# A forward Fourier step split 49 by 64 instead of 98 by 32, with products on quarters of TensorE's array

## The chip, the cores and the metric

One core of a Trainium2 chip runs the whole program. The metric is the device time of one execution in microseconds; lower is better. TensorE (PE in the profile) multiplies matrices, its weight loads are listed as PEld; VectorE is DVE, ScalarE is ACT, GpSimd is POOL, and SyncE (SP) issues all DMAs of this kernel.

## The reference

Eight sequences of 3136 rows and 256 columns go through a Fourier layer and then, row by row, through a two-matrix layer with a softmax-weighted activation. Cut to what matters:

```python
X = np.fft.rfft(x, axis=1)                       # x: (8, 3136, 256), along the 3136 rows
Yr = Xr @ w_r - Xi @ w_i + b_r
Yi = Xr @ w_i + Xi @ w_r + b_i
Y  = soft_threshold(Yr, 0.01) + 1j * soft_threshold(Yi, 0.01)
x  = np.fft.irfft(Y, n=3136, axis=1).reshape(25088, 256)
h  = x @ w_in                                    # w_in: 256 x 1024
solu = h * softmax(h)
ln = (solu - mean(solu)) / sqrt(var(solu) + 1e-6) * g_ln
out = ln @ w_out                                 # w_out: 1024 x 256
```

## The kernel before

The transform of one sequence is made of matrix products. The 3136 row numbers are split in two factors, and the forward part has two steps: step 1 transforms along the first factor, its result goes through DRAM (`s1`), and step 2 applies the second factor together with the twiddles. Then the mixing with `w_r` and `w_i` follows (`mix`), the inverse step 1 (`inv1`), DRAM again (`s2`), and the inverse step 2 (`inv2`), which writes columns of 98 rows into a ring in SBUF (`ring_hi`, `ring_lo`). From the ring, tiles of 128 rows are taken by the second layer: `moe_head` (first product, softmax), `moe_turn` (split into two float16 parts and transposes by DMA, `th<-lh` and `tl<-ll`) and `moe_tail` (second product, `po`, and the output).

Numbers are held as pairs of float16, high and low, and a product is three matmuls: high by high, high by low, low by high. Only the first sequences are treated otherwise: step 1 and 2 of sequences 0 and 1 are in float32 (`fwd1_plain`).

In step 1 a sequence is eight chunks of four values of the second factor, 98 rows by 1024 elements. `fwd1` loads one chunk (`xt`, one DMA of 98 rows of 4 KB), splits it in `xh` and `xl` (ScalarE, VectorE), and for each half of 512 columns makes three matmuls of 98 rows into one PSUM bank. ScalarE and VectorE bring each bank to SBUF as the pair `av`, and one DMA of 98 rows of 4 KB stores it. Before its eight chunks a sequence is read once more in eight loads of 128 rows for the largest absolute value (`load_peak`, `set_scales`). `xt` has four buffers, shared by both.

`inv1` already works on halves of the array: its weights `gb` have 64 rows, and the two products of a pair of frequencies stand on the two row halves.

Nothing in the program runs in the order of the text. `Plan` records every operation with a key, and `order` builds the order of each engine's queue: at each point it takes, of the operations that could start within 50 ns of the first, the one with the smallest key. It works with lengths for each operation (`weigh`), a single transfer bus and a fixed charge for entering and leaving a split array. All operations of the kernel are issued at one line, so in the profile nearly everything stands at L342, and groups are told apart by the tiles' names (`fa_s` there is also `fa16_s`, since digits are left out). Keys count tiles of the second layer. The main loop has, for each sequence `b`, 24 or 25 such tiles; beside them it spreads the front of sequence `b + 2` (`front_a`: peaks, scales, `fwd1`) and the second half of the front of `b + 1` (`front_b`: `fwd2`, `mix`, `inv1`):

```python
if b + 2 < B:
    front_a(b + 2, first + 6, (L - 6) / 17)
if b + 1 < B:
    front_b(b + 1, first + (6 if b == 0 else 0), (L - (8 if b == 0 else 2)) / (NU + 3))
```

At the start nothing else can run: sequence 0 goes through `fwd1_plain` in eight chunks, all are stored, and `fwd2` begins when its first `bin` has been loaded back.

Of the kernel before, what the change touches and what calls it, by code (L numbers as in the profile page):

```python
# [25 lines left out]
H = N1 // 2  # L26
Q = (H - 1) // 2
# [5 lines left out]
S_SCALE, B_SCALE, Z_SCALE, X_SCALE = 2.0**-7, 2.0**-5, 2.0**-11, 2.0**-11  # L33
# [6 lines left out]
def fft_constants():  # L40

    FA, IA = np.zeros((N1, N1)), np.zeros((N1, N1))
    comps = []
    for q in range(Q):
        comps += [(2 * q + 1, 0), (2 * q + 2, 0), (2 * q + 1, 1), (2 * q + 2, 1)]
    comps += [(0, 0), (H, 0)]  # L50
    for c, (k1, im) in enumerate(comps):
        t = 2 * np.pi * ((np.arange(N1) * k1) % N1) / N1
        FA[:, c] = -np.sin(t) if im else np.cos(t)
        IA[c, :] = (1.0 if k1 in (0, H) else 2.0) / S * (-np.sin(t) if im else np.cos(t))

    def angle(k):
        return 2 * np.pi * ((np.arange(N2)[:, None] * np.asarray(k)[None, :]) % S) / S

    P = 4 * N2
    FB, GB = np.zeros((P, Q, P)), np.zeros((P, Q, P))  # L60
    for q in range(Q):
        for j in range(2):
            k = 2 * q + 1 + j + N1 * np.arange(N2)
            s = np.where(2 * k > S, -1.0, 1.0)[None, :]
            C, Sn = np.cos(angle(k)), np.sin(angle(k))
            re, im = slice(j * N2, (j + 1) * N2), slice((2 + j) * N2, (3 + j) * N2)
            FB[re, q, re], FB[im, q, re] = C, Sn
            FB[re, q, im], FB[im, q, im] = -Sn * s, C * s
            GB[re, q, re], GB[im, q, re] = C.T, -(Sn * s).T
            GB[re, q, im], GB[im, q, im] = Sn.T, (C * s).T  # L70
    kd, kn = N1 * np.arange(1, N2 // 2), H + N1 * np.arange(N2 // 2)
    nd, m = len(kd), len(kd) + len(kn)
    FS, GS = np.zeros((2 * N2, P)), np.zeros((P, 2 * N2))
    d, n, I = slice(0, N2), slice(N2, 2 * N2), 2 * N2
    alt = np.cos(np.pi * np.arange(N2))
    FS[d, 0:nd], FS[n, nd:m], FS[d, m], FS[d, m + 1] = np.cos(angle(kd)), np.cos(angle(kn)), 1.0, alt
    FS[d, I : I + nd], FS[n, I + nd : I + m] = -np.sin(angle(kd)), -np.sin(angle(kn))
# [12 lines left out]
    out = dict(fa=FA.astype(np.float32), fbf=FB.astype(np.float32), fsf=FS.astype(np.float32))  # L90
    out["iaf"] = (IA * IA_SCALE).astype(np.float32)
    parts = dict(fa16=FA * A_SCALE, fb=FB, fs=FS, gb=GB * G_SCALE, gs=GS * G_SCALE, ia=IA * IA_SCALE)
# [132 lines left out]
class Op:  # L225
    def __init__(self, engine, key, seq):
        self.engine, self.key, self.seq = engine, key, seq
        self.calls, self.length, self.moved, self.tiles = [], 0.0, 0.0, []
        self.needs, self.next, self.start, self.end, self.half, self.port = set(), [], None, None, False, False
# [7 lines left out]
class Plan:  # L237
# [60 lines left out]
    def weigh(self, op, name, args, kw, ins, outs):  # L298
# [45 lines left out]
    def order(self):  # L344
        ready = {e: [] for e in self.ENGINES}
        free = dict.fromkeys(self.ENGINES, 0.0)
        waits, bus, half, port = {}, 0.0, False, 0.0
# [35 lines left out]
        while len(done) < len(self.ops):  # L383
# [68 lines left out]
def fft_mix_solu_kernel(ctx: ExitStack, tc, x, w_r, w_i, b_r, b_i, w_in, w_out, g_ln, fa, fbf, fsf, iaf, fa16, fb, fs, gb, gs, ia, out):  # L452
# [70 lines left out]

    def load_after(t, src, before):
# [56 lines left out]
    def fwd1(b, c):  # L581
        if c == 0:
            s1[b] = dram.tile([N1, N2, 2, D], F16, name="s1")
        xt = xp.tile([P, C1], F32, name="xt", bufs=4)[:N1]
        nc.sync.dma_start(xt, x[b].rearrange("(n1 n2) d -> n1 (n2 d)", n1=N1)[:, c * C1 : (c + 1) * C1])
        xh = xp.tile([N1, C1], F16, name="xh")
        xl = xp.tile([N1, C1], F16, name="xl")
        k = scales[b]["x"][:N1]
        nc.scalar.activation(xh, xt, AF.Copy, scale=k)
        nc.vector.scalar_tensor_tensor(xl, xt, k, xh, ALU.mult, ALU.subtract)  # L590
        n2 = C1 // D
        av = xp.tile([P, n2, 2, D], F16, name="av")[:N1]
        for h in range(C1 // HF):
            hs = slice(h * HF, (h + 1) * HF)
            pa = front_psum(b)
            nc.reserve(av[:, h * HF // D : (h + 1) * HF // D])
# [3 lines left out]
            pv = pa[:N1].rearrange("p (n d) -> p n d", d=D)  # L600
            ah, al = (av[:, h * HF // D : (h + 1) * HF // D, j] for j in range(2))
# [6 lines left out]
    def fwd1_plain(b, c):  # L608


        if c == 0:
            s1[b] = dram.tile([N1, N2, D], F32, name="s1f")
        n2 = C1 // D
        pool, name, bufs = (mp, "u", 4) if b == 0 and c % 2 == 0 else (xp, "xt", 4)
        xt = pool.tile([P, C1], F32, name=name, bufs=bufs)[:N1]
        if b and c < 4:
# [18 lines left out]
        for av, i, n in parts:  # L635
            nc.sync.dma_start(s1[b][:, c * n2 + i : c * n2 + i + n], av.rearrange("p (n d) -> p n d", d=D))
# [8 lines left out]
    def load_bin(b, g):  # L645

        if b >= PLAIN:
            v = s1[b][: 4 * Q].rearrange("(q c) n t d -> q c n (t d)", c=4).rearrange("q c n m -> (c n) q m")
# [3 lines left out]
        v = s1[b][: 4 * Q].rearrange("(q c) n d -> q (c n) d", c=4).rearrange("q r d -> r q d")  # L652
# [15 lines left out]
    def fwd2(b, u):  # L668
# [3 lines left out]
        if n == 1:  # L672
            if b >= PLAIN:
                bt, gi, fw = fp.tile([K, 1, 2, D], F16, name="bin_s", bufs=1), 0, [fs_s]
                nc.sync.dma_start(bt[:, 0], s1[b][4 * Q :].rearrange("c n t d -> (c n) t d"))
            else:
                bt, gi, fw = fp.tile([K, 1, D], F32, name="bin_s", bufs=1), 0, [fsf_s]
                nc.sync.dma_start(bt[:, 0], s1[b][4 * Q :].rearrange("c n d -> (c n) d"))
# [353 lines left out]
    fa16_s = load([N1, 2, N1], fa16, "fa16_s", dtype=F16)  # L1032
# [132 lines left out]
    for b in range(B):  # L1165
        tiles = range(0, 24) if b % 2 == 0 else range(24, 49)
        L = len(tiles)
        if b == 0:
            front_a(1, -40, 0.5)
        if b + 2 < B:  # L1170
            front_a(b + 2, first + 6, (L - 6) / 17)
        if b + 1 < B:
            front_b(b + 1, first + (6 if b == 0 else 0), (L - (8 if b == 0 else 2)) / (NU + 3))
        groups = 0
        for n, t in enumerate(tiles):
            need = min((t + 1) * P - (b % 2) * S, S)
            while groups < N2 // G2 and groups * G2 * N1 < need:
                nc.key = first + n - 2
# [6 lines left out]
            nc.key = first + n + 1  # L1185
# [30 lines left out]
```

## Time and profile before

| what | value |
|---|---|
| median of 3 runs | 1636.32 us (1631.87 to 1637.99) |
| the profiled execution | 1638.51 us |
| its span, first to last instruction | 1636.7 us |
| TensorE busy | 1586.2 us, 97% |
| VectorE busy | 1317.3 us, 80% |
| ScalarE busy | 1234.6 us, 75% |
| GpSimd busy | 1129.3 us, 69% |
| DMA: time of packets, share of 16 engines | 80.9% |
| mean granted TensorE clock | 0.986 |

The span is cut in 40 slices of 40.9 us in the page; a digit is the busy share of a slice in tenths. A matmul's duration in the lists runs past the start of the next one, so the cost of a stream of matmuls is read from the distances of their starts. A row of a window gives its length, the busy time and count of each engine, the granted clock, the DMA share and GB/s.

### The profile page before, as it was taken

How to read it: one execution, taken by the hardware profiler on the slowest of the kernel's cores; microseconds unless marked ns; L12 is line 12 of the kernel's file. 1: busy time of each engine (PE TensorE's matmuls, PEld its weight loads, DVE VectorE, ACT ScalarE, POOL GpSimd, SP SyncE). 2: the span in 40 equal slices, each digit the busy share in tenths (PEclk: the TensorE clock that was granted, in tenths of full speed). 3: DMA queues.
4: the chain of work that ended last, by engine and by line, in shares of the span. 5: the costliest groups of instructions: out<-in, count | busy, mean ns of one | idle time of the engine just before them, and what ended most of it. 6: DMA issues, size and time to landing. Idle time of an engine off the chain costs nothing.

```text
span 1636.7 us, 37871 instructions
## 1 busy us (share of the span) xinstructions
PE 1586.2 (97%) x13040; PEld 1127.8 (69%) x13040; DVE 1317.3 (80%) x3343; ACT 1234.6 (75%) x2496; POOL 1129.3 (69%) x1889
## 2 busy tenths in 40 slices
PE   6979999999999999999999999999999999999998
PEld 3545877676775787668766677766877677676675
DVE  4778779985888867997799977899689877777774
ACT  4667678885788767887678867788678876678786
POOL 0656777676875687768766687766887677776775
PEclk8989999999999999999999999999999999999999
DMA  8868966997669977899758996699767977669776
GB/s 249 274 223 205 194 149 155 229 207 146 151 151 233 214 152 133 189 249 192 162 102 191 251 209 132 134 234 243 162 134 158 191 165 145 119 137 144 150 130 106
DMA packets 532258, 290.23 MB, mean 177 GB/s; under 512 B 425978, under 2 KB 502300, under 8 KB 532064
## 3 DMA queue, kind: packets, MB, share of 16 engines
q1 hardware_dynamic: 532064, 287.81, 80.9%
q8 instruction: 102, 1.67, 0.4%
q14 instruction: 92, 0.75, 0.1%
HBM read 107.89 MB, written 77.07 MB: 113 GB/s over the span
## 4 chain that ended last, share of the span: by engine, by line
PE 78%; DMA 8%; DVE 5%; ACT 3%; POOL 2%; issue 2%; SPq 0%; DVEq 0%; ACTq 0%; POOLq 0%
PE po L342 26%; PE ph L342 24%; PE pf L342 23%; PE pb L342 4%; DMA th<-lh 4%; DMA tl<-ll 3%; DVE u L342 1%; POOL ll L342 1%; ACT junk L342 1%; DVE xl L342 1%; ACT lh L342 1%; DVE nm L342 1%; ACT u L342 0%; DMA zt<-s 0%; DVE av L342 0%
## 5 line engine op out<-in xcount | busy, mean ns | idle before, releaser
L342 POOL TENSOR_TENSOR ll<-u,lh 128x1024 f16<-128x1024 f32 x196 | 427.2, 2180 | 116.0 <-ACT lh L342 110.0
L342 PE MATMUL po<-wout,th 128*128 128x256 f16 x3136 | 375.3, 273 | 10.6 <-DMA th<-lh 9.2
L342 PEld LDWEIGHTS <-th 128*128 128x128 f16 x3136 | 303.8, 98 | 74.5 <-DMA th<-lh 15.8
L342 ACT ACTIVATE u<-ph,m,hsb 128x512 f32<-128x512 f32 x384 | 296.1, 776 | 50.5 <-DVE m L342 46.9
L342 DVE TENSOR_REDUCE nm<-ph 128x1 f32<-128x512 f32 x392 | 265.0, 684 | 82.3 <-PE ph L342 80.7
L342 DVE SCALAR_TENSOR_TENSOR u<-ph,ch,u 128x512 f32<-128x512 f32 x392 | 281.6, 747 | 31.1 <-ACT u L342 20.0
L342 PE MATMUL ph<-win_hi,ring_hi 128*128 128x512 f16 x784 | 298.2, 380 | 1.3 <-DVE ring_lo L342 0.8
L342 PE MATMUL ph<-win_low,ring_lo 128*128 128x512 f16 x784 | 297.8, 380 | 0.0
L342 PE MATMUL ph<-win_lo,ring_hi 128*128 128x512 f16 x784 | 297.8, 380 | 0.0
L342 ACT CAST lh<-u 128x1024 f16<-128x1024 f32 x196 | 205.3, 1047 | 64.2 <-DVE u L342 57.2
L342 PEld LDWEIGHTS <-ring_hi 128*128 128x128 f16 x1568 | 150.3, 98 | 142.7 <-issue 5.9
L342 ACT ACTIVATE junk<-u,total 128x1024 bf16<-128x1024 f32 x196 | 226.0, 1153 | 13.1 <-POOL total L342 12.8
L342 PE MATMUL po<-wout,tl 128*128 128x256 f16 x1568 | 204.2, 273 | 6.3 <-DMA tl<-ll 6.3
L342 PEld LDWEIGHTS <-tl 128*128 128x128 f16 x1568 | 150.4, 98 | 39.8 <-DMA tl<-ll 8.6
L342 POOL TENSOR_TENSOR y<-yt,yc 128x512 f32<-128x512 f32 (+1 forms) x104 | 133.0, 1279 | 61.0 <-ACT yt L342 32.7
L342 POOL TENSOR_TENSOR yl<-y,yh 128x512 f16<-128x512 f32 (+1 forms) x104 | 127.2, 1224 | 47.6 <-ACT yh L342 47.0
L342 PE MATMUL pf<-w_hi,Xh 128*128 128x256 f16 (+1 forms) x546 | 149.2, 273 | 0.0
L342 PE MATMUL pf<-w_hi,Xl 128*128 128x256 f16 (+1 forms) x546 | 148.8, 273 | 0.0
L342 PE MATMUL pf<-w_lo,Xh 128*128 128x256 f16 (+1 forms) x546 | 148.8, 273 | 0.0
L342 ACT ACTIVATE o<-po,r 128x256 f32<-128x256 f32 x196 | 92.6, 473 | 72.0 <-PE po L342 53.8
L342 PEld LDWEIGHTS <-ring_lo 128*128 128x128 f16 x784 | 76.7, 98 | 93.8 <-DVE ring_lo L342 0.8
L342 PEld LDWEIGHTS <-Xh 128*128 128x128 f16 (+1 forms) x1196 | 114.2, 99 | 27.7 <-issue 3.7
(189 smaller groups left out, 2851.0 us busy)
## 6 DMA issues: line engine op xcount, KB each, us to landing
xt<-in_x_dram SPq DMA_DIRECT2D x108, 392.0 KB
zt<-s SPq DMA_DIRECT2D x56, 392.0 KB
s<-zout SPq DMA_DIRECT2D x42, 512.0 KB
s<-av SPq DMA_DIRECT2D x48, 392.0 KB
bin<-s SPq DMA_DIRECT2D x36, 512.0 KB
out_dram<-o SPq DMA_DIRECT2D x64, 98.0 KB
bin<-s1f SPq DMA_DIRECT2D x12, 512.0 KB
s1f<-av SPq DMA_DIRECT2D x10, 392.0 KB
```

The source lines that it names most:

```text
L342: getattr(engine, name)(*args, **kw)
```

## The change

The forward split becomes 49 by 64; the inverse keeps 98 by 32. Step 1's matrix is 49 by 49. In float32 (`fwd1_plain`) two copies of it stand on the diagonal of a 98 by 98 matrix, so that a matmul still takes 98 rows: two sets of 49. In float16 (`fwd1`) a chunk of 1024 elements is laid on partitions 0 to 48 and 64 to 112, and four products, each of 49 rows into 64 output rows by 512 columns, stand on the four quarters of the array; three rounds of four matmuls fill two PSUM banks, each bank both its halves of partitions. ScalarE and VectorE then work on 113 partitions, with as many instructions as before.

Each load of a chunk and each store becomes two DMAs of 49 rows (in `fwd1` the load has two runs of 2 KB in each row). The x buffers become one constant tile of four places: in the float16 stages places 0 and 1 for `fwd1`, 2 and 3 for the peaks; partitions 32 to 63 of the first two are cleared once (`clear_between`). Step 2 keeps its sizes: a group is now two components by 64 values, not four by 32. In the planner the array may be split in 1, 2 or 4, and four keys change.

```diff
-S, N1, N2 = 3136, 98, 32
-H = N1 // 2
-Q = (H - 1) // 2
+F1, F2 = N1 // 2, 2 * N2
+Q = (F1 - 1) // 2
...
-            op.half = "gb" in ins[0].tile.kw["name"]
-            op.length += n / 2 if op.half else n
+            op.split = {"gb": 2, "fa16_s": 4}.get(...)
+            op.length += n / op.split
...
-                if op.half != half:
-                    at += 100.0 if op.half else 220.0
-                half = op.half
+                if op.split != split:
+                    at += 100.0 if split == 1 else 220.0
+                split = op.split
...
+    places = const.tile([P, 4, C1], F32, name="xt")
...
+    def clear_between():
+        nc.gpsimd.memset(places[P // 4 : P // 2, :2], 0.0)
...
-        t = xp.tile([P, C1], F32, name="xt", bufs=4)[:, :n]
+        t = x_place(2, 3)[:, :n]
...
     def fwd1(b, c):
-        xt = xp.tile([P, C1], F32, name="xt", bufs=4)[:N1]
-        nc.sync.dma_start(xt, x[b].rearrange("(n1 n2) d -> n1 (n2 d)", n1=N1)[:, c * C1 : (c + 1) * C1])
+        half = P // 2
+        R = half + F1
+        xt = x_place(0, 1)[:R]
+        xv = x[b].rearrange("(n1 c g r i) d -> c r n1 g (i d)", n1=F1, g=2, r=2, i=2)
+        for r in range(2):
+            nc.sync.dma_start(xt[r * half : r * half + F1].rearrange("p (g m) -> p g m", g=2), xv[c, r])
...
-        for h in range(C1 // HF):
-            pa = front_psum(b)
-            with nc.together():
-                for i, (t, j) in enumerate(((xh, 0), (xh, 1), (xl, 0))):
-                    nc.tensor.matmul(pa[:N1], fa16_s[:, j], t[:, hs], start=i == 0, stop=i == 2)
+        pa = [front_psum(b) for _ in range(2)]
+        with nc.together():
+            for i, (t, j) in enumerate(((xh, 0), (xh, 1), (xl, 0))):
+                for r in range(2):
+                    rows = slice(r * half, r * half + F1)
+                    for g in range(2):
+                        nc.tensor.matmul(
+                            pa[r][g * half : (g + 1) * half], fa16_s[rows, j], t[rows, g * HF : (g + 1) * HF], start=i == 0, stop=i == 2
+                        )
...
-        nc.sync.dma_start(s1[b][:, c * n2 : (c + 1) * n2], av)
+        for g in range(2):
+            nc.sync.dma_start(
+                s1[b][:, 8 * c + 4 * g : 8 * c + 4 * g + 4].rearrange("k n t d -> k (n t d)"),
+                av[g * half : g * half + F1].rearrange("p r i t d -> p (r i t d)"),
+            )
...
     def fwd1_plain(b, c):
-        nc.sync.dma_start(xt, x[b].rearrange("(n1 n2) d -> n1 (n2 d)", n1=N1)[:, c * C1 : (c + 1) * C1])
+        xv = x[b].rearrange("(n1 h c n2) d -> c h n1 (n2 d)", n1=F1, h=2, n2=n2)
+        for h in range(2):
+            nc.sync.dma_start(xt[h * F1 : (h + 1) * F1], xv[c, h])
...
-            nc.sync.dma_start(s1[b][:, c * n2 + i : c * n2 + i + n], av.rearrange("p (n d) -> p n d", d=D))
+            for h in range(2):
+                at = h * N2 + c * n2 + i
+                nc.sync.dma_start(s1[b][:, at : at + n].rearrange("k n d -> k (n d)"), av[h * F1 : (h + 1) * F1])
...
         if b + 2 < B:
-            front_a(b + 2, first + 6, (L - 6) / 17)
+            front_a(b + 2, first + 9, (L - 9) / 17)
         if b + 1 < B:
-            front_b(b + 1, first + (6 if b == 0 else 0), (L - (8 if b == 0 else 2)) / (NU + 3))
+            front_b(b + 1, first + (6 if b == 0 else -0), (L - (8 if b == 0 else 4)) / (NU + 3))
...
-                nc.key = first + n - 2
+                nc.key = first + n - 3
                 inv2(b, groups)
...
-            nc.key = first + n + 1
+            nc.key = first + n + 1.5
             moe_tail(*turned.pop(0))
```

More of the change, by code (lines that the diff above doesn't have):

```diff
@@ L40, in fft_constants, with angle @@
 def fft_constants():
[L46 to L50, printed above, removed]
+    FA, IA = np.zeros((F1, F1)), np.zeros((N1, N1))
+    for c, (k1, im) in enumerate([(q + 1, im) for q in range(Q) for im in range(2)] + [(0, 0)]):
+        t = 2 * np.pi * ((np.arange(F1) * k1) % F1) / F1
+        FA[:, c] = -np.sin(t) if im else np.cos(t)
+    comps = [(q + 1 + j * F1, im) for q in range(Q) for im in range(2) for j in range(2)] + [(0, 0), (F1, 0)]
     for c, (k1, im) in enumerate(comps):
         t = 2 * np.pi * ((np.arange(N1) * k1) % N1) / N1
[L53 to L57, printed above, removed]
+        IA[c, :] = (1.0 if k1 in (0, F1) else 2.0) / S * (-np.sin(t) if im else np.cos(t))
+    def angle(k, n2=N2):
+        return 2 * np.pi * ((np.arange(n2)[:, None] * np.asarray(k)[None, :]) % S) / S
     P = 4 * N2
@@ L88, in fft_constants @@
     GS = GS.reshape(2, 2 * N2, 2 * N2).transpose(1, 0, 2)
-    out = dict(fa=FA.astype(np.float32), fbf=FB.astype(np.float32), fsf=FS.astype(np.float32))
+    both = np.zeros((2 * F1, 2 * F1))
+    both[:F1, :F1] = both[F1:, F1:] = FA
+    quarters = np.zeros((P // 2 + F1, P // 2))
+    quarters[:F1, :F1] = quarters[P // 2 :, :F1] = FA
+    out = dict(fa=both.astype(np.float32), fbf=FB.astype(np.float32), fsf=FS.astype(np.float32))
     out["iaf"] = (IA * IA_SCALE).astype(np.float32)
-    parts = dict(fa16=FA * A_SCALE, fb=FB, fs=FS, gb=GB * G_SCALE, gs=GS * G_SCALE, ia=IA * IA_SCALE)
+    parts = dict(fa16=quarters * A_SCALE, fb=FB, fs=FS, gb=GB * G_SCALE, gs=GS * G_SCALE, ia=IA * IA_SCALE)
     out.update({k: halves(v) for k, v in parts.items()})
@@ L228, in __init__ @@
         self.calls, self.length, self.moved, self.tiles = [], 0.0, 0.0, []
-        self.needs, self.next, self.start, self.end, self.half, self.port = set(), [], None, None, False, False
+        self.needs, self.next, self.start, self.end, self.split, self.port = set(), [], None, None, 1, False
     def touch(self, tile):
@@ L307, in weigh @@
             n = moving.cells.size * (4 if moving.dtype == F32 else 1) * 0.42 + 1
-            op.half = "gb" in ins[0].tile.kw["name"]
-            op.length += n / 2 if op.half else n
+            op.split = {"gb": 2, "fa16_s": 4}.get(ins[0].tile.kw["name"].rstrip("0123456789" if "gb" in ins[0].tile.kw["name"] else ""), 1)
+            op.length += n / op.split
         else:
@@ L346, in order @@
         free = dict.fromkeys(self.ENGINES, 0.0)
-        waits, bus, half, port = {}, 0.0, False, 0.0
+        waits, bus, split, port = {}, 0.0, 1, 0.0
         for op in self.ops:
@@ L522, in fft_mix_solu_kernel, with x_place @@
     s1 = {}
+    places = const.tile([P, 4, C1], F32, name="xt")
+    turns = {}
+    def x_place(*some):
+        turns[some] = turns.get(some, -1) + 1
+        return places[:, some[turns[some] % len(some)]]
+    def clear_between():
+        nc.gpsimd.memset(places[P // 4 : P // 2, :2], 0.0)
     def load_after(t, src, before):
@@ L589, in fwd1 @@
+        xv = x[b].rearrange("(n1 c g r i) d -> c r n1 g (i d)", n1=F1, g=2, r=2, i=2)
+        for r in range(2):
+            nc.sync.dma_start(xt[r * half : r * half + F1].rearrange("p (g m) -> p g m", g=2), xv[c, r])
+        xh = xp.tile([P, C1], F16, name="xh")[:R]
+        xl = xp.tile([P, C1], F16, name="xl")[:R]
+        k = scales[b]["x"][:R]
         nc.scalar.activation(xh, xt, AF.Copy, scale=k)
         nc.vector.scalar_tensor_tensor(xl, xt, k, xh, ALU.mult, ALU.subtract)
-        n2 = C1 // D
@@ L592, in fwd1 @@
-        av = xp.tile([P, n2, 2, D], F16, name="av")[:N1]
-        for h in range(C1 // HF):
-            hs = slice(h * HF, (h + 1) * HF)
-            pa = front_psum(b)
-            nc.reserve(av[:, h * HF // D : (h + 1) * HF // D])
-            with nc.together():
-                for i, (t, j) in enumerate(((xh, 0), (xh, 1), (xl, 0))):
-                    nc.tensor.matmul(pa[:N1], fa16_s[:, j], t[:, hs], start=i == 0, stop=i == 2)
-            pv = pa[:N1].rearrange("p (n d) -> p n d", d=D)
-            ah, al = (av[:, h * HF // D : (h + 1) * HF // D, j] for j in range(2))
+        av = xp.tile([P, 2, 2, 2, D], F16, name="av")[:R]
@@ L602, in fwd1 @@
+        for r in range(2):
+            pv = pa[r][:R].rearrange("p (n d) -> p n d", d=D)
+            ah, al = av[:, r, :, 0], av[:, r, :, 1]
             nc.scalar.activation(ah, pv, AF.Copy, scale=S_SCALE / A_SCALE)
             nc.vector.scalar_tensor_tensor(al, pv, S_SCALE / A_SCALE, ah, ALU.mult, ALU.subtract)
-        nc.sync.dma_start(s1[b][:, c * n2 : (c + 1) * n2], av)
+        for g in range(2):
[3 more added lines that the diff above has]
+            )
@@ L611, in fwd1_plain @@
         if c == 0:
-            s1[b] = dram.tile([N1, N2, D], F32, name="s1f")
+            s1[b] = dram.tile([F1, F2, D], F32, name="s1f")
         n2 = C1 // D
-        pool, name, bufs = (mp, "u", 4) if b == 0 and c % 2 == 0 else (xp, "xt", 4)
-        xt = pool.tile([P, C1], F32, name=name, bufs=bufs)[:N1]
-        if b and c < 4:
+        xt = (mp.tile([P, C1], F32, name="u", bufs=4) if b == 0 and c % 2 == 0 else x_place(0, 1, 2, 3))[:N1]
+        early = b and c < 4
+        if early:
             nc.hold(raw[0, 4])
-        nc.sync.dma_start(xt, x[b].rearrange("(n1 n2) d -> n1 (n2 d)", n1=N1)[:, c * C1 : (c + 1) * C1])
+        xv = x[b].rearrange("(n1 h c n2) d -> c h n1 (n2 d)", n1=F1, h=2, n2=n2)
+        for h in range(2):
+            if h and early:
+                nc.hold(raw[0, 4])
+            nc.sync.dma_start(xt[h * F1 : (h + 1) * F1], xv[c, h])
         note_peak(b, c, N2 // n2, xt)
```

36 lines of the change are left out of this document (18 added, 18 removed).

## The prediction

> **What bounds the kernel now.** I read the page first: busy shares, the slices, the chain that ended last.
>
> ```profile
> PE 1586.2 (97%) x13040; PEld 1127.8 (69%) x13040; DVE 1317.3 (80%) x3343; ACT 1234.6 (75%) x2496; POOL 1129.3 (69%) x1889
> ...
> DVE  4778779985888867997799977899689877777774
> ...
> DMA  8868966997669977899758996699767977669776
> ...
> PE 78%; DMA 8%; DVE 5%; ACT 3%; POOL 2%; issue 2%; SPq 0%; DVEq 0%; ACTq 0%; POOLq 0%
> ```
>
> TensorE is the bound: 97% busy and 78% of the chain. But VectorE and the DMA engines have six stretches near 9 tenths, and these are where the edited function, float16 step 1 (`fwd1`), runs for sequences 2 to 7. So I asked for busy times by window, one line for each of these six stages (DMA share and GB/s stand last), with one quiet stretch between two stages, and then for the chain inside each stage, in the same order.
>
> ```profile
> 255.00:318.00 63.00, 63.00 (x457) 42.59 (x455) 57.87 (x133) 50.56 (x99) 43.25 (x61) 1.00 0.81 200
> 460.00:522.00 62.00, 57.93 (x429) 38.33 (x428) 56.77 (x133) 51.30 (x101) 42.06 (x68) 0.98 0.89 195
> 655.00:713.00 58.00, 58.00 (x449) 38.53 (x447) 56.04 (x130) 48.87 (x94) 40.05 (x60) 1.00 0.89 212
> 850.00:915.00 65.00, 64.56 (x504) 42.54 (x503) 60.39 (x149) 56.53 (x110) 42.13 (x68) 1.00 0.85 191
> 1050.00:1110.00 60.00, 59.18 (x440) 38.44 (x439) 57.72 (x130) 50.41 (x101) 42.19 (x67) 1.00 0.95 223
> 1110.00:1240.00 130.00, 129.88 (x1195) 97.69 (x1193) 106.66 (x280) 98.84 (x206) 99.30 (x169) 1.00 0.82 172
> 1240.00:1300.00 60.00, 60.00 (x475) 40.52 (x473) 55.71 (x137) 52.35 (x102) 39.56 (x68) 1.00 0.83 178
> ```
> ```profile
> by line: PE pf L342 38.1%; PE ph L342 29.2%; PE po L342 22.0%; DMA th<-lh 14.3%; issue 3.1%; ACT av L342 1.8%; ACT lh L342 1.6%; ACT junk L342 0.0%; ACTq L342 0.0%
> by line: PE pf L342 28.8%; PE ph L342 25.4%; PE po L342 20.4%; DMA zt<-s 12.8%; DVE xl L342 4.0%; issue 2.9%; SPq L342 2.5%; DVE av L342 1.3%; DVE u L342 1.2%; DVE c L342 0.3%; DVE ch L342 0.2%; DVE nm L342 0.2%; DVEq L342 0.0%
> by line: PE pf L342 35.5%; PE ph L342 30.5%; PE po L342 27.5%; ACT u L342 2.5%; ACT junk L342 2.0%; ACT lh L342 1.8%; issue 0.8%; ACTq L342 0.1%; ACT av L342 0.1%
> by line: PE pf L342 21.6%; PE ph L342 13.8%; PE po L342 12.8%; DMA tl<-ll 10.7%; DMA th<-lh 9.4%; issue 5.8%; DMA xt<-in_x_dram 4.3%; POOL ll L342 4.0%; ACT lh L342 3.2%; ACT u L342 3.0%; DVE u L342 2.4%; DVE xl L342 2.0%; ACT junk L342 1.7
> by line: PE pf L342 12.5%; DVE xl L342 11.2%; DVE av L342 9.4%; PE po L342 9.1%; DVE u L342 8.4%; DVE nm L342 7.3%; PE ph L342 6.7%; issue 6.4%; DMA s<-av 6.2%; ACT junk L342 3.8%; ACT lh L342 3.4%; DVE ring_lo L342 3.3%; DVE peaks L342 3.0
> by line: PE pf L342 36.6%; PE ph L342 32.9%; PE po L342 30.9%
> ```
>
> TensorE's share of the chain is 89, 75, 93, 48, 28 and 100%, a mean of 72%. In the fourth and fifth stages time saved on TensorE is mostly not on the path: there VectorE (57.72 of 60 us) and transfers end the waits.
>
> **The products of step 1.** Now 288 matmuls of 98 rows by 512 columns; then 576 of 49 rows on quarters.
>
> ```profile
> L342 PE MATMUL pf<-xh,fa_s 98*98 98x512 f16 x192 | 57.4, 380 | 0.0
> L342 PE MATMUL pf<-xl,fa_s 98*98 98x512 f16 x96 | 36.3, 378 | 0.0
> ```
> ```profile
> 1456.09 0.39 PE L342 MATMUL pf<-yh,gb 64*128 64x256 f16 x4
> ...
> 1457.19 0.38 PE L342 MATMUL pf<-yh,gb 64*128 64x256 f16 x4
> 1457.51 1.92 PE L342 MATMUL po<-wout,th 128*128 128x256 f16 x16
> 1459.27 1.04 PE L342 MATMUL po<-wout,tl 128*128 128x256 f16 x8
> 1460.14 0.38 PE L342 MATMUL ph<-win_hi,ring_hi 128*128 128x512 f16 x1
> 1460.36 0.38 PE L342 MATMUL ph<-win_lo,ring_hi 128*128 128x512 f16 x1
> ...
> 1462.51 0.38 PE L342 MATMUL ph<-win_low,ring_lo 128*128 128x512 f16 x1
> 1462.82 0.40 PE L342 MATMUL pf<-yh,gs_s 64*64 64x256 f16 x2
> ```
>
> Durations overlap, so I go by starts. The twelve ph matmuls of 512 columns from 1460.14 to 1462.51 start 0.216 us apart, so 288 take 62.2 us. The kernel already puts two products on halves of the array: 24 gb matmuls of 256 columns fill 1456.09 to 1457.51, 1.42 us, while 16 + 8 po matmuls of 256 columns take 2.63 us (1457.51 to 1460.14). So two products do run at once, at half of 2.63, 1.31 us, and 0.11 us is left over for leaving the mode. Entering a tiled mode shows where gs_s begins 0.31 us after a 0.216 us matmul: 0.1. No row shows four at once. Ends: 0.65 us a chunk (four at once, 12 x 0.054) and 1.30 us (two at once, as now). I take 0.65, by the gb row, where two gave all of their factor. Saved 31.1 us, less 48 entries and exits of 0.21, 10.1: 21.0 us of TensorE time, 3.5 a stage. Times 72%: **-15 us** on the path (ends -21 and, with two at once, +10).
>
> A rule of the Trainium skill speaks against the four: "TensorE: Matmul & The Clock Gate", section "Part 3: Packing small matmuls — row/col tiling", says a weight load overlaps matmuls in flight only when its row group differs, and two quarters share each row group. By that rule this term is about +10. The ph rows do not bear it out: each has its own weights in the same rows and still starts 0.216 us after the one before.
>
> ScalarE and VectorE work per chunk is as before in width (512 or 1024 elements): zero. Two PSUM banks are now taken at once and their four evacuations follow together; between 0 and 0.65 us of latency a chunk, hidden behind the other tiles' work; if that cover goes, 48 x 0.65 = 31. The x buffers are two for `fwd1` and two for the peaks, not four shared; counted with the transfers. `clear_between` is one POOL memset of 2048 elements, once:
>
> ```profile
> L342 POOL TENSOR_TENSOR ll<-u,lh 128x1024 f16<-128x1024 f32 x196 | 427.2, 2180 | 116.0 <-ACT lh L342 110.0
> ```
>
> at most twice that, 4.4 us, and hidden, since its first readers belong to the first of the six stages. fp32 step 1 keeps its 98-row matmuls and step 2 its 128-deep ones: zero.
>
> **The transfers.** Every 98-row load of x and every store of step 1's result becomes two of 49 rows, and x for `fwd1` comes in runs of 2 KB, not 4.
>
> ```profile
> L342 SPq DMA_DIRECT2D xt<-in_x_dram x108: 321/378/2529, 1.6 to 1268.2; - x108
> ```
> ```profile
> 3.00:15.00 12.00, 12.00 (x39) 6.14 (x39) 7.45 (x7) 5.85 (x10) 0.00 (x0) 1.00 0.92 267
> 16.00:20.00 4.00, 4.00 (x13) 1.83 (x12) 2.16 (x4) 3.83 (x9) 2.67 (x4) 1.00 1.00 348
> 34.80:37.00 2.20, 0.46 (x2) 0.46 (x3) 0.00 (x0) 0.00 (x0) 0.00 (x0) 0.50 1.09 372
> ```
> ```profile
> 1.22 0.34 SPq L342 DMA_DIRECT2D u<-in_x_dram  x1
> ...
> 4.30 0.39 SPq L342 DMA_DIRECT2D xt<-in_x_dram  x1
> ```
> ```profile
> 29.19 3.38 DMA s1f<-tl
> 32.63 3.86 DMA bin<-s1f
> ...
> 36.54 56.88 PE pb L342 x376
> ```
>
> Issues: eight chunks of eight sequences, so 64 loads and 66 stores more (two chunks are stored in halves) at 0.38 us: 49 us on SP's queue over the span, 6 in a stage, with the transposes queued behind them. SP has nothing else to do but wait for data, so zero; if its queue were full, 6 a stage.
>
> Bandwidth is the term that I think decides. Between 3 and 15 us eight x loads of 98 rows were queued at once (issued 1.22 to 4.30) and moved 267 GB/s; loads of 128 rows moved 348 to 372. That is 2.7 GB/s per row, and 2.7 to 2.9: the rate goes with the rows of one transfer, and queueing several did not lift it. So I expect 133 GB/s of 49-row transfers. (The Trainium skill has a reason, "DMA: Bandwidth & Descriptors", section "Why a DMA increments its semaphore by 16 and not by 1": a transfer uses the largest number of engines up to 16 that divides its rows, so 14 for 98 and 7 for 49; by it the rate halves too, and 267 against 372 points the same way.)
>
> At the start the first sequence's 3.2 MB in and 3.2 MB out take 24 us at 267 GB/s, from 1.22 to the last landing at 32.57, and TensorE then waits for `bin` until 36.54. At 133 GB/s they take 48. Ends: 0 (halves side by side) and +24. I take **+20**: the row rate, less the 4 us of other loads at 16 to 20, which can go beside.
>
> In each of the six stages the same 6.4 MB takes 48 us of some engines' time and not 24, and these had 5 to 19% of some 60 us free, 3 to 12 us. So 12 to 21 us of lateness can pile up; the stretches after (share 0.82 of 130 us) drain it. It costs where an x load, a transpose or a zt load comes after its reader. Transfers hold 9, 8, 0, 16, 4 and 0 us of the six chains (14.3% of 63, and so on), 6 a stage. I take a third more of that, **+12** in all; ends 0 and +13 a stage.
>
> **The order.** inv2 goes out one tile earlier, the tail half a tile later, `fwd1` is squeezed into fewer tiles.
>
> ```profile
> PE po L342 <- DMA th<-lh: 9.2, 10, 2.0
> ...
> PE po L342 <- DMA tl<-ll: 6.3, 6, 2.3
> PE pf L342 <- DMA zt<-s: 4.1, 1, 4.1
> ```
>
> At best all 19.6 us of these waits go; at worst the denser `fwd1` meets VectorE, which has 2.3 us free in the fifth stage: +5 in all. I take a quarter of the waits, **-5**, since transfers come later as well. What is late next is then x for `fwd1`, with ScalarE's in-order work behind it.
>
> **Sum.** -15 + 20 + 12 - 5 = +12 on the profiled 1638.5 us (span 1636.7): 1650.5. That execution lies 2.2 above the median 1636.3, so **1648**.
>
> **Rivals.**
> 1. *The halves run side by side* (the other side). If two 49-row transfers in flight use different engines, the start costs about +2 and the stages 0: -15 - 5 + 2, or with -21 for the products where the order lets TensorE have it: 1618 to 1612, I name 1617. For it: the bytes are the same, and three stages have TensorE on 93 to 100% or near it. Against: the eight queued loads at 267. It decides as soon as start and stages together cost less than 12.
> 2. *It cancels.* The start loses 20, but the stages absorb all lateness, as after 1110 where the chain is nearly all TensorE: -15 - 5 + 20 = 0: 1636.
> 3. *Only two quarters at once.* Then -15 becomes +10: 1648 + 25 = 1673. For it: nothing shows four; against: the ph and gb rows.
>
> **How the numbers follow.** Forecast 0.36 (its own range 1640 to 1675), rival 1 0.34, rival 2 0.22, rival 3 0.08. About 0.5% (8 us) is what a measurement of this kernel tells from no change. Faster 0.34, same 0.22, slower 0.36 + 0.08 = 0.44. The range runs from a good rival 1 (-21 - 9 + 2: 1608) to rival 3 with one more us a stage, the last 4 us of the start and the +5 of the order (1673 + 6 + 4 + 5: 1688).
>
> **What would show it.** Right: the matmuls on quarters start 0.054 us apart and twelve take under 0.9 us; the first `bin<-s1f` issues near 52 us, not 32.63; GB/s between 3 and 15 falls well under 200; a lower TensorE share of the chains in the six stages. Wrong: the first `bin` load still near 33, or more PE waits for th, tl and zt than 19.6 us with the start unchanged, or starts 0.108 us apart.

## The result and the profile after

The changed kernel takes 1741.2 us (median of 4 runs, 1736.2 to 1746.5) against 1634.2 us of the kernel before in the same comparison: a ratio of 1.0653 [1.0608, 1.0697], 107 us slower. The forecast was 1648 with a range of 1608 to 1688. The profiled execution has a span of 1742.7 us (before 1636.7) and a mean granted clock of 0.969 (before 0.986).

The page of the changed kernel, the same parts as shown of before: busy shares, the DMA slices, and the chain of work that ended last.

```profile
PE 1601.3 (92%) x13328; PEld 1109.0 (64%) x13328; DVE 1333.1 (76%) x3343; ACT 1237.0 (71%) x2496; POOL 1124.7 (65%) x1890
...
DMA  5768997999989985798757995499864996658876
...
PE 53%; DMA 16%; ACT 5%; DVE 3%; issue 3%; SPq 2%; POOL 2%; ACTq 0%; DVEq 0%; POOLq 0%
```

TensorE has fallen from 78% to 53% of the chain, and transfers have doubled from 8% to 16%. Yet TensorE's busy time rose by 15 us, though step 1 needs less of it: its matmuls became slower somewhere. Both have to be explained.

**The start.** Busy times between 3 and 15 us of the changed kernel, then the first readback of step 1's result on SP, the first matmul on it, and the first second-layer tile in the list of tile `ph` (the figure before "to" is when it starts; the kernel before first, then the changed one).

```profile
3.00:15.00 12.00, 11.29 (x34) 5.80 (x33) 4.96 (x5) 4.45 (x8) 0.00 (x0) 1.00 0.45 177
```
```profile
43.70 0.94 SPq L348 DMA_DIRECT2D bin<-s1f  x2
```
```profile
47.68 4.78 PE L348 MATMUL pb<-fbf,bin 128*128 128x128 f32 x24 [14.93 <-DMA bin<-s1f]
```
```profile
L342 PE MATMUL ph<-win_hi,ring_hi x784: 376/379/634, 120.3 to 1618.4; 128*128 128x512 f16 x196
L348 PE MATMUL ph<-win_hi,ring_hi x784: 376/379/634, 137.6 to 1726.2; 128*128 128x512 f16 x196
```

The transfers moved 177 GB/s where whole 98-row loads moved 267, with a DMA share of 0.45 (0.92 before) although loads were queued without a gap: 0.45 of sixteen engines is 7.2. The trace's packet records say the same: seven data packets are under way at once for 87% of this time, where the kernel before had fourteen or more. They also show why half the engines did not halve the rate: a 4 KB packet took 159 ns in the median, and 222 before. The readback issues 11.1 us later, and the first second-layer tile starts at 137.6 us; in the kernel before it started at 120.3. So 17 us are lost at the start.

**The rest.** I take the part from the first `ph` matmul of the second layer to that of the last sequence's first tile, 120.3 to 1482.9 us before and 137.6 to 1587.4 after, first row before, second row after.

```profile
120.30:1482.90 1362.60, 1344.52 (x11398) 969.73 (x11398) 1135.60 (x2900) 1049.62 (x2133) 977.96 (x1637) 1.00 0.82 176
```
```profile
137.60:1587.40 1449.80, 1353.36 (x11661) 948.16 (x11660) 1149.04 (x2893) 1048.10 (x2127) 973.44 (x1634) 0.98 0.82 166
```

It is 87 us longer: 78 us more of TensorE idle (96.4 against 18.1) and 9 us more of TensorE busy. Start, this part, and 1.5 us more in the tail make up the difference of the spans. Window rows for the six float16 stages of the changed kernel, placed by hand over the stretches where step 1's matmuls run, as those of before were:

```profile
295.00:360.00 65.00, 56.31 (x443) 33.67 (x441) 54.39 (x140) 48.65 (x92) 38.47 (x65) 0.95 0.94 187
505.00:580.00 75.00, 64.70 (x537) 38.77 (x534) 61.17 (x154) 59.30 (x112) 41.19 (x79) 1.00 0.92 169
708.00:775.00 67.00, 56.82 (x458) 33.85 (x457) 49.16 (x119) 50.12 (x95) 38.40 (x66) 0.95 0.92 160
928.00:1004.00 76.00, 61.95 (x463) 35.18 (x460) 53.39 (x141) 53.57 (x102) 38.48 (x70) 0.91 0.98 176
1133.00:1200.00 67.00, 57.52 (x458) 34.20 (x455) 51.86 (x127) 51.16 (x100) 37.90 (x67) 0.92 0.93 170
1345.00:1422.00 77.00, 64.26 (x535) 38.82 (x533) 59.49 (x147) 56.13 (x112) 44.33 (x78) 0.96 0.94 168
```

Together they last 427 us with 362 of TensorE busy; the six stages of before (their six rows stand in the prediction) lasted 368 with 363. So 59 of the 87 us lie inside these windows and 28 between them. The DMA engines show a higher busy share than before (0.92 to 0.98, against 0.81 to 0.95) and move less (160 to 187 GB/s, against 178 to 223). The clock has dropped too: 1 less the clock, times the length, sums to 21 us here and to 1 us before.

Who waits is told by TensorE's waits, and by the one of ScalarE that is new:

```profile
PE po L348 <- DMA th<-lh: 37.1, 24, 3.8
PE po L348 <- DMA tl<-ll: 27.1, 21, 3.7
PE pf L348 <- DMA zt<-s: 18.9, 9, 4.2
```
```profile
ACT xh L348 <- DMA xt<-in_x_dram: 22.8, 15, 4.8
```

The two transposes and `zt` took 19.6 us of TensorE before; now 83.1. In the chain inside the fourth stage (928 to 1004 us) they are nearly half, and SP's queue, which issues them, is another 15.5%:

```profile
by line: DMA tl<-ll 26.9%; DMA th<-lh 21.0%; SPq L348 15.5%; PE po L348 7.5%; issue 5.6%; PE ph L348 4.6%; ACT junk L348 3.3%; ACT u L348 3.0%; POOL r L348 2.8%; PE pf L348 2.0%; DMA out_dram<-o 1.7%; ACT zout L348 1.5%; ACT xh L348 1.4%; A
```

And such a wait costs more than itself. TensorE's timeline in the third stage, and the window of the stretch that follows:

```profile
733.09 1.05 PE L348 MATMUL po<-wout,tl 128*128 128x256 f16 x8 [2.36 <-DMA tl<-ll]
733.98 0.38 PE L348 MATMUL ph<-win_hi,ring_hi 128*128 128x512 f16 x1
734.19 0.58 PE L348 MATMUL ph<-win_lo,ring_hi 128*128 128x512 f16 x1
734.57 0.63 PE L348 MATMUL ph<-win_low,ring_lo 128*128 128x512 f16 x1
734.99 0.63 PE L348 MATMUL ph<-win_hi,ring_hi 128*128 128x512 f16 x1
735.42 0.63 PE L348 MATMUL ph<-win_lo,ring_hi 128*128 128x512 f16 x1
735.85 0.63 PE L348 MATMUL ph<-win_low,ring_lo 128*128 128x512 f16 x1
736.41 1.07 PE L348 MATMUL pf<-xh,fa_s 49*64 49x512 f16 x8
737.26 0.58 PE L348 MATMUL pf<-xl,fa_s 49*64 49x512 f16 x4
737.77 0.39 PE L348 MATMUL ph<-win_hi,ring_hi 128*128 128x512 f16 x1
738.00 0.38 PE L348 MATMUL ph<-win_lo,ring_hi 128*128 128x512 f16 x1
```
```profile
734.20:737.70 3.50, 3.50 (x18) 0.92 (x16) 0.69 (x1) 0.45 (x1) 0.07 (x1) 0.51 1.16 163
```

After a wait of 2.36 us for a transpose, the `ph` matmuls soon start 0.42 to 0.43 us apart, twice the usual 0.216, in a stretch of 3.5 us at a granted clock of 0.51; then they are back at 0.22. (The Trainium skill describes this, "TensorE: Matmul & The Clock Gate", section "HAM oscillation — how this bites in real kernels": idle gaps over about 3.4 us, such as waits on DMAs, throttle the clock to half, again and again. This trace agrees on the half, 0.51, but not on the length: here a gap of 2.36 us was enough.)

It is no single case. In the clock records of the part from 137.6 to 1587.4 us, half the clock was granted in 15 stretches of 3.4 or 6.8 us, 61 us together, and each came behind an idle gap of TensorE of 2.2 to 4.2 us; of the 21 gaps over 2 us, 15 were followed by one. In the same part of the kernel before there is one such stretch, of 6.8 us. Half of the difference, 27 us, is what the clock took.

**The quarters** did what was forecast. One chunk on TensorE's timeline, between two products of the second layer:

```profile
297.70 0.63 PE L348 MATMUL pf<-xh,fa_s 49*64 49x512 f16 x8
298.16 0.39 PE L348 MATMUL pf<-xl,fa_s 49*64 49x512 f16 x4
298.48 1.05 PE L348 MATMUL po<-wout,tl 128*128 128x256 f16 x8
```

Twelve matmuls of 512 columns from 297.70 to 298.48, 0.78 us with the switching (the median of the 48 chunks is 0.77), against 1.30 for the six whole ones.

### The profile page after: what moved, and what is told of

Same layout as the page of the kernel before. It is cut to its first block, busy times and chain, and to the rows that moved or that the text cites. A ratio compares the mean times of both kernels' runs of the same rounds, so it can differ in the third digit from the quotient of the medians.

```text
span 1742.7 us, 38708 instructions
## 1 busy us (share of the span) xinstructions
PE 1601.3 (92%) x13328; PEld 1109.0 (64%) x13328; DVE 1333.1 (76%) x3343; ACT 1237.0 (71%) x2496; POOL 1124.7 (65%) x1890
## 4 chain that ended last, share of the span: by engine, by line
PE 53%; DMA 16%; ACT 5%; DVE 3%; issue 3%; SPq 2%; POOL 2%; ACTq 0%; DVEq 0%; POOLq 0%
PE po L348 19%; PE ph L348 17%; PE pf L348 17%; DMA tl<-ll 7%; DMA th<-lh 5%; SPq L348 2%; DMA xt<-in_x_dram 2%; DMA zt<-s 2%; ACT junk L348 1%; ACT lh L348 1%; ACT u L348 1%; DVE u L348 1%; POOL ll L348 1%; ACT av L348 1%; POOL r L348 1%
## 5 line engine op out<-in xcount | busy, mean ns | idle before, releaser
L348 POOL TENSOR_TENSOR ll<-u,lh 128x1024 f16<-128x1024 f32 x196 | 421.6, 2151 | 183.3 <-ACT lh L348 152.5
L348 PE MATMUL po<-wout,th 128*128 128x256 f16 x3136 | 382.0, 276 | 44.9 <-DMA th<-lh 37.1
L348 PE MATMUL ph<-win_hi,ring_hi 128*128 128x512 f16 x784 | 303.2, 387 | 2.7 <-ACT o L348 1.4
L348 PE MATMUL ph<-win_low,ring_lo 128*128 128x512 f16 x784 | 302.3, 386 | 0.0
L348 PE MATMUL ph<-win_lo,ring_hi 128*128 128x512 f16 x784 | 302.2, 385 | 0.0
L348 PEld LDWEIGHTS <-ring_hi 128*128 128x128 f16 x1568 | 150.8, 99 | 148.7 <-issue 22.8
L348 PE MATMUL po<-wout,tl 128*128 128x256 f16 x1568 | 207.4, 276 | 27.3 <-DMA tl<-ll 27.1
L348 POOL TENSOR_TENSOR yl<-y,yh 128x512 f16<-128x512 f32 (+1 forms) x104 | 122.5, 1178 | 33.3 <-ACT yh L348 31.4
```

Source lines behind the costliest of these rows:

```text
L348: getattr(engine, name)(*args, **kw)
```

## The experiments

Differences in microseconds are the ratio less 1, times the 1630.6 to 1634.7 us of the kernel before in the same comparison. The theory: a transfer of 49 rows uses fewer DMA engines, is slower, and crowds those that the transposes need. Its rivals: the number of transfers, the planner's order with the new keys, and the quarters themselves.

**1 and 2. The kernel before, with its transfers cut in two.** Only the loads of step 1's chunks and the stores of its results change, as 49 + 49 rows or as 56 + 42:

```diff
-        nc.sync.dma_start(s1[b][:, c * n2 : (c + 1) * n2], av)
+        for lo, hi in ((0, 49), (49, 98)):        # second kernel: (0, 56), (56, 98)
+            nc.sync.dma_start(s1[b][lo:hi, c * n2 : (c + 1) * n2], av[lo:hi])
...                                        # and likewise the loads of x
```

> The kernel before, with nothing changed but that each 98-row load of x for step 1 and each 98-row store of its result is issued as two transfers of 49 rows. Theory A (a 49-row transfer moves at half the rate of a 98-row one, and queued halves share the same engines): most of the loss comes back, some 60 to 100 us slower than before, the first bin load 10 to 12 us later, and 3 to 15 us of the start at about 180 GB/s. Theory B (it is the number of transfers on SP's queue): the same, and 56 + 42 rows as slow as this. Theory C (the loss comes from the moved keys and the two x buffers): within 10 us of before.

> As the one above, but the two transfers have 56 and 42 rows. As many transfers more on SP's queue, but by the Trainium skill (DMA: Bandwidth & Descriptors, on why a DMA increments its semaphore by 16) both row counts divide by 14, the number of engines that 98 rows get. Theory A: within 10 us of before. Theory B: as slow as 49 + 49. Theory C: within 10 us of before, like 49 + 49.

49 + 49: 1714.9 us, ratio 1.0508 [1.0475, 1.0540], +83. 56 + 42: 1639.4 us, 1.0031 [1.0013, 1.0050], +5. The same number of transfers, issues and bytes. Their windows from 3 to 15 us, 49 + 49 first:

```profile
3.00:15.00 12.00, 10.23 (x33) 4.63 (x32) 4.88 (x4) 4.10 (x7) 0.00 (x0) 1.00 0.45 173
```
```profile
3.00:15.00 12.00, 12.00 (x40) 5.83 (x40) 7.32 (x6) 5.90 (x11) 0.00 (x0) 1.00 0.92 246
```

So the rows of a transfer decide, and twice the transfers alone cost 5 us. The DMA share is that of seven engines in the one and of nearly fifteen in the other. (That is the rule of the Trainium skill named in the prediction, "DMA: Bandwidth & Descriptors", section "Why a DMA increments its semaphore by 16 and not by 1": 49 gives 7, while 56 and 42 both give 14.)

**3. The kernel before with 96 + 2 rows,** the same edit with (0, 96), (96, 98).

> The kernel before with its 98-row loads of x and stores of step 1 as 96 + 2 rows (16 engines and 2, not 14). If the share of engines is what counts, a little faster than before, 0 to 10 us, though with twice as many transfers; 56 + 42 rows were 5 us slower. If the number of transfers counts: 5 us slower again.

1640.5 us, 1.0045 [1.0032, 1.0058], +7: a first part of 96 rows brings nothing here over the 98 whole ones.

**4. The changed kernel with transfers of 48 rows.** Each pair of 49 + 49 becomes 48 + 48 and one transfer for the two rows that are left over, in all stages:

```diff
-            nc.sync.dma_start(xt[h * F1 : (h + 1) * F1], xv[c, h])
+            nc.sync.dma_start(xt[h * F1 : (h + 1) * F1 - 1], xv[c, h, : F1 - 1])
...
+        nc.sync.dma_start(xt[F1 - 1 :: F1], xv[c, :, F1 - 1])
...                                        # the stores and float16 step 1 likewise
```

> The changed kernel, with each pair of 49-row transfers replaced by two of 48 rows and one small one for the last row of both halves: half as many transfers again. Theory A (48 rows get 16 engines): most of the 107 us come back, the start is as short as before or shorter, and the quarters' 21 us of TensorE time begin to show: 1610 to 1640 us. Theory B: as slow as the changed kernel or slower, 1741 to 1780. Theory C: 1741.

1633.8 us, 1.0009 [0.9994, 1.0025]: all but 1 us of the 107 is gone, with the quarters and the new keys kept. Its start is still late, though:

```profile
L348 PE MATMUL ph<-win_hi,ring_hi x784: 376/379/634, 139.6 to 1615.6; 128*128 128x512 f16 x196
```
```profile
PE pb L348 <- DMA u<-in_x_dram: 5.9, 1, 5.9
```

The first second-layer tile comes at 139.6 us: TensorE waits 5.9 us for its first chunk, which it did not before. Three transfers a chunk cost at the start about what the two slow ones did (19 and 17 us), and what follows is 18 us better than before.

**5 and 6. The start mended as well, and the start alone.** In the float32 step the two copies of the matrix are interleaved instead of stacked, so that its 98 rows stand in their order in memory and one transfer moves them; the first kernel also has the 48-row transfers in the float16 stages, the second keeps 49 rows there:

```diff
-both[:F1, :F1] = both[F1:, F1:] = FA
+both[0::2, 0::2] = both[1::2, 1::2] = FA
```

> The changed kernel with 48 + 48 rows and one transfer for the two last rows in the float16 stages, and with the float32 stages (the start) back to one transfer of 98 rows per chunk, by laying the two 49 by 49 matrices interleaved and not one after the other. Theory A, with what the first four runs showed (48 + 1 rows bring the time back to the level of before, but its first second-layer tile still begins at 139.6 us, not 120.3): the start's 17 to 19 us come back, 1610 to 1622 us, below both kernels. If the late start is not from its transfers: 1634.

> The changed kernel with only the float32 stages back to one transfer of 98 rows. Theory A: it gains what the start lost, 17 to 25 us, and the six float16 stages stay long: 1715 to 1725 us, with the first second-layer tile near 120 us. If most of the loss came through the start (a late beginning that later stages carry on): 1650.

Both mended: 1623.6 us (1622.7 to 1627.6), 0.9949 [0.9934, 0.9965], 8 us faster than before: it beats both kernels. Start alone: 1724.1 us, 1.0560 [1.0532, 1.0588], so the start is worth some 15 us and the other 91 lie in the float16 stages. TensorE's waits and the first tile of the first of them:

```profile
PE po L348 <- DMA th<-lh: 5.3, 5, 2.4
...
PE pf L348 <- DMA zt<-s: 3.0, 4, 1.2
...
PE po L348 <- DMA tl<-ll: 2.1, 4, 0.8
```
```profile
L348 PE MATMUL ph<-win_hi,ring_hi x784: 376/379/634, 120.7 to 1606.5; 128*128 128x512 f16 x196
```

Against the changed kernel, the waits for the `th` transposes fall from 37.1 to 5.3 us, for `tl` from 27.1 to 2.1 and for `zt` from 18.9 to 3.0, with nothing changed but rows of transfers, the float32 layout, and the order that the planner makes of them.

**7, 8 and 9. The keys.** The changed kernel with the four old keys, experiment 5 with them, and the kernel before with the new ones:

```diff
-front_a(b + 2, first + 9, (L - 9) / 17)
+front_a(b + 2, first + 6, (L - 6) / 17)
...                     # front_b: L - 4 to L - 2; inv2: n - 3 to n - 2; moe_tail: n + 1.5 to n + 1
```

> The changed kernel with the four keys of the kernel before. Theories A and B: still 60 us or more above before; the moved keys give transfers more time, so without them it is somewhat slower, 1741 to 1770. Theory C: 1640 to 1680.

> The version with 48 + 48 rows in the float16 stages, one 98-row transfer per chunk in the float32 stages, and the four keys of the kernel before. With 49-row transfers the old keys were 15 us faster than the new (1725.7 against 1741.2). If the new keys are simply worse: 1605 to 1618 us. If they only lost to the crowded engines there: 1623 or slower, up to 1632.

> The kernel before with the four new keys and nothing else. My prediction gave them -5 us (between -20 and +5). If the denser float16 step 1 meets VectorE: 0 to 10 us slower. If the earlier inv2 and later tail take away waits for transfers: 0 to 10 us faster.

1725.7 us, 1.0579 [1.0541, 1.0616]: the old keys are 12 us better in the changed kernel (a weak difference: the intervals of the two ratios just overlap). In experiment 5 they are 32 us worse (1655.8 us, 1.0145 [1.0105, 1.0185]). In the kernel before the new ones change nothing (1633.5 us, 1.0008 [0.9993, 1.0023]). The keys have no worth of their own; it depends on the transfers, with either sign.

**10. What TensorE time in step 1 is worth.** The kernel before with two of the three products (the low part of x by the matrix's high part is left out), 96 matmuls fewer, 20.7 us at 0.216:

```diff
-for i, (t, j) in enumerate(((xh, 0), (xh, 1), (xl, 0))):
+for i, (t, j) in enumerate(((xh, 0), (xh, 1))):
```

> The kernel before with the third product of float16 step 1 (low part of x by high part of the matrix) left out: 96 matmuls of 0.216 us, 20.7 us of TensorE time less, about what the quarters save, and nothing else changed. If TensorE's time in these stages is on the path as the chain says (72%): 12 to 18 us faster. If VectorE or the transfers hold the stages: 0 to 6 us faster.

1626.9 us, 0.9964 [0.9949, 0.9978]: 20.7 us less of TensorE is 6 us of time (4 to 8), 28% and not 72%. This kernel was planned anew too, so the 28% holds for the work taken away and the order made for what is left.

**11 and 12. Loads or stores.** Experiment 5 with 48 rows only in the float16 loads, and only in the float16 stores; the other direction keeps 49:

> Changed kernel, float32 stages with 98-row transfers, float16 stages with the loads of x at 48 rows and the stores still at 49. Between 1724 (both at 49) and 1624 us (both at 48). If the occupied engines count: about half, 1660 to 1685, and the same for the stores. If it is the late x load itself, with two buffers, on which ScalarE and VectorE wait: near 1630 here, and near 1720 for the stores alone.

> As the one above with the two the other way round: stores at 48 rows, loads at 49. Occupied engines: 1660 to 1685 us. The late x load: near 1720. If a store that is late in leaving its av buffer is what counts: near 1630.

48-row loads with 49-row stores: 1687.3 us, 1.0343 [1.0291, 1.0396], +56. 48-row stores with 49-row loads: 1635.8 us, 1.0023 [0.9998, 1.0048], +4. Beside experiment 5 (-8), 49-row stores cost 64 us and 49-row loads 12. But each kernel was planned anew, and experiments 7 to 9 showed what an order can do.

**13 to 18. The same with the order held.** The planner's order stays as it is; only when a transfer is issued is it cut in two. The changed kernel with 48 + 1 rows for each 49, in both directions, loads only, stores only; and the kernel before with 49 + 49 for 98, likewise:

```diff
 for name, args, kw in op.calls:
...
+    if name == "dma_start" and len(args) == 2 and args[0].shape[0] == args[1].shape[0] == 49 and (True):
+        for lo, hi in ((0, 48), (48, 49)):
+            engine.dma_start(args[0][lo:hi], args[1][lo:hi])
+        continue
...       # one direction: a condition in place of True; the kernel before: 98 and ((0, 49), (49, 98))
```

> The changed kernel with its planned order untouched, operation by operation; only when a 49-row transfer is issued, it goes out as 48 rows and 1 row. Against the changed kernel (1741.2) nothing differs but the engines that a transfer uses, and the added small ones. If the engines alone cost what the 48-row versions gained: at most 1650 us. If those gained by their other order too: 1660 to 1700.

> As s_both, but only the loads of x go out as 48 + 1 rows; the stores keep 49, in the same order. Loads and stores move the same bytes over the same engines: if occupied engines alone count, loads and stores each bring back about half of what s_both does (some 1690 to 1700). If the stores really cost more, as a_loads (1687) against a_stores (1636) seemed to say: little, 1710 to 1740.

> As s_both, but only the stores go out as 48 + 1 rows. Occupied engines alone: 1690 to 1700. Stores cost more: 1650 to 1665.

> The kernel before with its planned order untouched; each 98-row load of x and store of step 1 goes out as two of 49 rows. Engines alone: as slow as b_49_49, 1700 to 1730. If b_49_49's own order had a part in its 82 us: below 1690.

> The kernel before, its issue order left as planned; only the stores of step 1's results go as 49 + 49 rows, the loads of x stay whole (both together cost 87 us in this control). If stores of 49 rows carry the cost whatever the order (as in the changed kernel, where lengthening the stores' rows brought 47 us and the loads' 2): 1695 to 1715. If that was a matter of the changed kernel's order alone, stores and loads share it: 1660 to 1690.

> The same with only the loads of x as 49 + 49 rows, the stores whole. If stores carry the cost: 1634 to 1655, of it some 10 us at the start. If both share it: 1660 to 1690.

| order held | 98 or 49 rows cut in | median | ratio | us |
|---|---|---|---|---|
| changed kernel | 48 + 1, both | 1688.4 | 1.0336 [1.0313, 1.0359] | +55 |
| changed kernel | 48 + 1, loads | 1742.8 | 1.0665 [1.0633, 1.0697] | +109 |
| changed kernel | 48 + 1, stores | 1693.8 | 1.0365 [1.0338, 1.0391] | +60 |
| kernel before | 49 + 49, both | 1721.3 | 1.0533 [1.0493, 1.0573] | +87 |
| kernel before | 49 + 49, stores | 1687.4 | 1.0342 [1.0323, 1.0361] | +56 |
| kernel before | 49 + 49, loads | 1655.2 | 1.0140 [1.0118, 1.0162] | +23 |

With not one operation moved in the plan, cutting the transfers of the kernel before into 49 + 49 costs 87 us; so in that kernel it is the transfers, not the order made for them (26 of the 87 us are at the start, where the first `ph` tile comes at 146.0). That the number of transfers costs little rests on experiment 2 alone: 56 + 42 rows with the order held were not run. In the kernel before the two directions come near to adding up (56 + 23 = 79), and the last two kernels' first tiles show how much of each is the start, stores first:

```profile
L347 PE MATMUL ph<-win_hi,ring_hi x784: 376/379/634, 132.7 to 1666.4; 128*128 128x512 f16 x196
```
```profile
L347 PE MATMUL ph<-win_hi,ring_hi x784: 376/379/634, 130.6 to 1641.1; 128*128 128x512 f16 x196
```

That is 12 and 10 us at the start, so 44 and 13 in the rest. The last pair's expectations fit neither way alone: stores carry most, but loads have a share in this order. In the changed kernel's own order, 48 + 1 rows in both directions bring back 52 of the 107 us, the second case of the expectation. In the stores alone they bring 47 us, 4 of them at the start, and in the loads alone nothing. TensorE's waits say the same, loads cut into 48 + 1 first, stores second:

```profile
PE po L353 <- DMA th<-lh: 34.3, 23, 4.2
PE po L353 <- DMA tl<-ll: 33.8, 22, 4.2
```
```profile
PE po L353 <- DMA tl<-ll: 24.0, 18, 5.9
PE po L353 <- DMA th<-lh: 22.0, 18, 4.2
```

All three designs agree that in the float16 stages 49-row stores cost over three times as much as 49-row loads of the same bytes (64 and 12, in kernels planned anew; 44 and 13; 43 and nothing). Why is not settled: no run separates a store's place in SP's queue from its direction. Open too is what keeps the held order with 48 + 1 rows 54 us above experiment 4: that has three transfers a chunk and not four, and an order of its own.

The records of two traces show where the transposes lose their time. I pair the 342 transposes of the first 171 tiles in the kernel before and in experiment 16, which has the same order. From the end of the instruction that makes a transpose's data to its issue on SP, 1.3 us pass in the mean before and 2.4 with 49 + 49 rows; from the issue to the last packet, 3.8 and 4.1. So 1.1 of the 1.4 us more lie ahead of the issue, while SP is mostly issuing other transfers, and crowded engines behind the issue are the smaller part. What slows SP's queue, no run isolates.

## Why the prediction was wrong

The sum was -15 + 20 + 12 - 5. The step that failed is the third term, the six float16 stages.

1. **Stages, +12: 87 us in the part that holds them.** Half the engines was seen, and so was what would come late. The price was wrong: "I take a third more of that" scaled the chain's present share of transfers, a figure of a kernel whose transposes were mostly in time. Lateness does not pile up until a quiet stretch drains it: the transposes and `zt` come late, most of all in their issue on SP, and TensorE waits at once, 63.5 us more over the three waits. The text's own end was +13 a stage, 78 us, but its range gave this term only 6 us more; an end that is written down belongs in the range.
2. **The clock was not in the sum.** TensorE's busy time in that part rose by 9 us although the quarters took 25 from it (48 times 1.30 less 0.78), so some 34 us went into slower work; the clock accounts for 27 of it, 20 more than before in the six windows alone. Waits were priced at their length, when most gaps over 2 us here were followed by half the clock for 3.4 or 6.8 us.
3. **Start, +20: 17.** The size is right, but partly by luck, for the working is not: 49 rows moved 177 GB/s, 0.66 of the 267, not half, and the readback issued at 43.70 us and not near 52. That is 11 us late; the other 6 were lost between it and the first second-layer tile, which the working did not have. That the halves would run side by side (rival 1) is refuted by the 0.45.
4. **Products, -15.** TensorE's saving was 25 us, more than the 21 of the sum, and the third rival, two quarters at once, is out. But a share of the chain is no rate of exchange: 20.7 us less gave 6 us (experiment 10), presumably because the chain then runs over other work. By that rate the term is -7.
5. **Order, -5: no value of its own.** The same keys gave +12, -32 and +1 us. With the transfers mended, products and keys together gave 8 us in experiment 5, and in experiment 4 what follows the start was 18 us shorter.
6. **SP's issues at nothing**: about right for their number, since twice the transfers cost 5 us in experiment 2. But SP's queue was not free: with 49 + 49 rows most of the transposes' added delay arose there, 1.1 of 1.4 us. That x for `fwd1` would be late next was right: 22.8 us of ScalarE.

## What to carry to other kernels

Before a dimension is split, look at what it does to the rows of every transfer: factors that suit the array (49 for quarters) can leave a DMA on seven engines, and 48 + 48 with a small transfer for the rest, planned anew, won back all but 1 us here. Price a slower transfer by what comes late behind it, in the queue that issues it and on the engines, and by the clock that TensorE loses after its waits, not by its own share of the chain. Before crediting time saved on the busiest engine, take some of its work away in a run: here 28% of what was taken away reached the time.

## What the runs showed of the hardware

- Transfers of 49 rows moved 173 to 177 GB/s with a DMA share of 0.45, whole 98-row ones 267 with 0.92: half the engines gave two thirds of the rate, not half, as a 4 KB packet took 159 ns and not 222.
- Twelve matmuls of 512 columns on quarters took 0.78 us, entering and leaving the split included: four ran at once, though two of each four share their rows of the array.
- A wait of 2.36 us was followed by 3.5 us at a clock of 0.51; of 21 idle gaps of TensorE over 2 us, 15 were followed by half the clock for 3.4 or 6.8 us, and no shorter gap was.
